# Halved doubled loads, a second late row buffer and re-measured planner figures in a spectral-mix and expert-retrieval kernel

## The chip, the cores and the metric

The kernel runs on one core of a Trainium2 chip. The core has a matrix engine (PE, with its weight loads shown apart as PEld), a vector engine (DVE), a scalar engine (ACT), a general engine (POOL, which here issues the gathers) and a queue engine (SP, which issues the plain loads and stores); all transfers run on 16 DMA engines. The metric is device time in microseconds, the median of several runs of the whole program.

## The reference

x has 2048 rows of 576 numbers. The result is a gated sum of two branches of the same x:

```
g   = sigmoid((x * gate_w).sum(-1))
a   = irfft2(rfft2(x) * (w_r + 1j * w_i))
q   = x @ w_q                          # 32 heads, two halves of 128 each
i1  = argmax over 64 of q1 . k1,  i2 = argmax over 64 of q2 . k2
e   = 64 * i1 + i2                     # one of 4096 rows per head
b   = sum over heads of gelu(x . u[e]) * v[e]
out = g * a + (1 - g) * b
```

With one candidate for each head the softmax is one. Branch a is a two-dimensional Fourier filter, written as products with cosine and sine tables. Branch b needs, for each of 2048 rows and 32 heads, one row of u and one row of v.

## The kernel before

**Tiles.** x is cut into 16 tiles of 128 rows. For branch b the 32 heads are cut into 8 chunks of 4. A *group* is one tile and one chunk: 4 gathers (one for each head; a gather fetches 128 rows of 4608 bytes, u and v side by side), 4 dot products with x on DVE (line 496, `group`), a gelu on ACT (line 500), and then the sum of the 4 v rows. That sum is done on DVE (line 514, four multiply-adds) or, where `is_d` says so, on PE by four diagonal matrices (`dg`, line 524) and eight products of 288 columns. There are 128 groups. Tiles 0 to 9 (`E_T`) are early: their 80 groups run beside the scores. Tiles 10 to 15 (`L_SEQ`) are late: their 48 groups, in which PE groups and DVE groups alternate, run beside the Fourier branch.

**Scores.** For each chunk `build_m` multiplies w_q by the keys; `scores` multiplies x by that, and DVE and ACT find the index of the largest score. The products are done on numbers cut in two parts (`load_x` makes a high part on ACT, line 361, and a low part on DVE, line 362). The last 64 columns of x are loaded twice, onto partitions 0 to 63 and 64 to 127, in blocks of 512 rows: 20 loads.

**Fourier branch.** When all score work is over, its memory is given to the second half (`switch`). `fold` (16 tiles) brings x into the buffer BT. Ten `unit` calls then do the Fourier transform over rows, the filter (`f4`, `f5`) and the way back (`f6`, `unit_back`) for two of 16 residues at a time. When all units are through, `invert` (16 tiles) does the last transform with a second table (`fi[1]`, line 640) and `mix` (line 835) adds both branches and stores.

**Row buffers.** Gathers land in a ring of 12 buffers (`uv`, NG), which also serves the loads of x and w_q in the scoring part. After `switch` one more buffer (`uv2`, NG2) serves gathers alone. A buffer is taken when the gather is issued, and is free again when the last reader of its v row (DVE or PE) is through.

**The order.** Every instruction stands in a list of jobs with a due time (`at`) and an assumed duration. `Plan.order` goes through time: whenever an engine is free it takes, among the jobs whose inputs are there and for which a buffer is free, the one that is due first. The order that comes out of it is fixed in the program; on the chip each engine then works in that order and waits where an input is late. So the assumed durations move no instruction of themselves, they change the order. They come from `dve`, `act`, `pe` (a product of n columns) and `load`; a gather is assumed to hold the DMA engines for `move` = 1.65 us, one after another. The due times of the late half: T0 is 636.8 in the list's own time; the late groups are due at T0 + 10 + 6.6 n (TLAG, TGS); fold n at T0 - 15 + 1.3 FPACE n; unit k at T0 + 20.8 FPACE + 14 FPACE k; inverse n 4.2 FPACE apart behind the units.

Of the kernel before, what the change touches and what calls it, by code (L numbers as in the profile page):

```python
# [32 lines left out]
def _tables():  # L33
# [10 lines left out]
    def rows(fn, ds):  # L44
        return fn(2 * np.pi * np.outer(ds, k) / D)

    z = np.zeros((P, DF))
    ct = z.copy()
# [4 lines left out]
    fwd = np.stack([  # L53
        rows(np.cos, np.arange(0, 128)), rows(np.cos, np.arange(128, 256)), ct,
        -rows(np.sin, np.arange(0, 128)), -rows(np.sin, np.arange(128, 256)), -st,
    ])
    ck = np.full(DF, 2.0)
    ck[0] = ck[-1] = 1.0
    ck /= S * D

    def irows(fn, ks):
        return fn(2 * np.pi * np.outer(ks, k) / D) * ck[ks][:, None]

    ct = z.copy()
    ct[:33] = irows(np.cos, np.arange(256, 289))
    st = z.copy()
    st[64:96] = irows(np.sin, np.arange(256, 288))
    inv = np.stack([
        irows(np.cos, np.arange(0, 128)), irows(np.cos, np.arange(128, 256)), ct,
        irows(np.sin, np.arange(0, 128)), irows(np.sin, np.arange(128, 256)), st,  # L70
# [12 lines left out]
        "t_fi": c(np.concatenate([fwd, inv]).transpose(1, 0, 2)),  # L83
        "t_f4": c(f4),
        "t_f6": c(f6),
# [158 lines left out]
def pe(n):  # L244
    return max(0.25, n * 0.0018)
# [7 lines left out]
def tile_kernel(ctx, tc, xn, xT, wqT, kT, wri, uv, gw, t_kr, t_fi, t_f4, t_f6, t_io, out):  # L253
# [84 lines left out]
    gate = pp.tile([P, NT], F32, tag="gate", name="gate")  # L338
    gone = pp.tile([P, NT], F32, tag="gone", name="gone")
# [16 lines left out]
    def load_x(b, i, at, at2):  # L356
        st = buf("uv", ROW, view=lambda x: x[:, 0, :512])
        ld(load(P * 2048, 2048), at, lambda: nc.sync.dma_start(st.ap, xT[:, i, b * 512 : b * 512 + 512]), [st])
        hi = xts[i if i < 4 else 8][b]
        lo, r = (xts[4 + i][b], 0) if i < 4 else (hi, 64)  # L360
        ac(act(512), at2, lambda: actv(hi.ap, st.ap, AF.Copy), [hi], [st])
        dv(dve(512), at2, lambda: vt(lo.ap[r:], st.ap[r:], hi.ap[r:].bitcast(F32), ALU.subtract), [lo], [st, hi])
# [117 lines left out]
    def group(t, c, at, ahead, gate_by=()):  # L480
        rows = []
        for k in range(HPC):
            g = buf(("uv", "uv2"), ROW)
            h = c * HPC + k

            def go(g=g, h=h):
                on("POOL", nc.gpsimd.indirect_dma_start(  # L487
                    out=g.ap.rearrange("p a d -> p (a d)"), out_offset=None, in_=uv,
                    in_offset=bass.IndirectOffsetOnAxis(ap=ei[t // 2][:, t % 2, h : h + 1], axis=0)))
# [124 lines left out]
    for tag, pool, n in (  # L614
            ("t2", "ip", NT2), ("bt", "ip", 1), ("fi1", "ip", 1), ("krb", "ip", 1),
            ("uv2", "x2", NG2), ("xl", "x2", NT - NE), ("gr", "x2", 1),
            ("f5", "fp", 2), ("kr", "fp", 1), ("fi0", "fp", 1), ("t4", "fp", 2), ("t6", "fp", 2), ("w", "fp", 2)):
# [14 lines left out]
    fi = [buf("fi0", [P, 6, DF]), buf("fi1", [P, 6, DF])]  # L632
# [5 lines left out]
    ld(load(P * 6936, 4096), T0 + 8, lambda: nc.sync.dma_start(fi[0].ap, t_fi[:, 0:6, :]), [fi[0]])  # L638
    ld(0.5, T0 + 15, lambda: nc.sync.dma_start(gw2.ap, gw.partition_broadcast(P)), [gw2])
    ld(load(P * 6936, 4096), T0 + 90, lambda: nc.sync.dma_start(fi[1].ap, t_fi[:, 6:12, :]), [fi[1]])  # L640
# [23 lines left out]
    def f2(q, at):  # L664
        p = psum()

        def go():
            for r in range(2):
                for n, i in enumerate(((0, 1, 2), (3, 4, 2))[r]):
                    mm(p.ap[:, r, :DF], BT.ap[:, i, :, q], fi[0].ap[:, 3 * r + n, :], start=n == 0, stop=n == 2)  # L670

        plan("PE", 6 * pe(DF), at, go, [p], [fi[0], (BT, "q", q)] + [(BT, "in", t, i) for t in range(NT) for i in range(2)])
# [4 lines left out]
    def turns(k, at):  # L677
        t4 = buf("t4", [P, 3, P])
        t6 = buf("t6", [P, 5, P])
        ld(load(P * 1024, 1024), at - 8, lambda: nc.sync.dma_start(t4.ap[:, 0:2, :], t_f4[k]), [(t4, 0)])  # L680
        ld(load(P * 1024, 1024), at - 8, lambda: nc.sync.dma_start(t6.ap[:, 0:2, :], t_f6[k]), [(t6, 0)])
        ac(act(128), at - 2, lambda: actv(t4.ap[:, 2, :], t4.ap[:, 1, :], AF.Copy, scale=-1.0), [(t4, 1)], [(t4, 0)])
        ac(act(256), at - 2, lambda: actv(t6.ap[:, 2:5:2, :], t6.ap[:, 0:1, :].to_broadcast([P, 2, P]), AF.Copy), [(t6, 1)], [(t6, 0)])
        ac(act(128), at - 2, lambda: actv(t6.ap[:, 3, :], t6.ap[:, 1, :], AF.Copy, scale=-1.0), [(t6, 2)], [(t6, 0)])
        tabs[k] = t4, t6

    def f4(k2, X, at):
# [4 lines left out]
        t4, t6 = tabs[min(k2, 16 - k2)]  # L692
        a, b = (1, 2) if k2 <= 8 else (2, 1)
        p = psum()

        def go():
            T, x, o = t4.ap, X.ap, p.ap
            mm(o[:, 0, :DF], T[:, 0, :], x[:, 0, :], start=True, stop=False)
            mm(o[:, 0, :DF], T[:, a, :], x[:, 1, :], start=False, stop=True)
            mm(o[:, 1, :DF], T[:, 0, :], x[:, 1, :], start=True, stop=False)  # L700
            mm(o[:, 1, :DF], T[:, b, :], x[:, 0, :], start=False, stop=True)

        plan("PE", 4 * pe(DF), at, go, [p], [X, (t4, 0), (t4, 1)])
# [226 lines left out]
```

## Time and profile before

| | us |
|---|---|
| median of 3 runs (lowest, highest) | 991.58 (990.01, 991.66) |
| the profiled execution, its own time | 1001.24 |
| span of its trace, first to last instruction | 999.5 |
| DVE busy in the span | 916.7 |
| PE busy in the span | 904.4 |
| last score product on PE starts | 601.4 |
| first product of the folds | 628.6 |
| first inverse | 862.7 |
| last product of an inverse | about 973 |

The profiled execution is 9.7 us (1.0%) longer than the median of the runs. A page of the profile gives for each engine its busy time; matmuls are shown with a modelled end that overlaps the next one, so their mean duration is longer than their pace. A window view gives the busy time of each engine in a stretch, with the number of instructions in brackets. A view of waits says which engine sat idle until which other instruction was done. Times in the trace count from the first instruction.

### The profile page before, as it was taken

How to read it: one execution, taken by the hardware profiler on the slowest of the kernel's cores; microseconds unless marked ns; L12 is line 12 of the kernel's file. 1: busy time of each engine (PE TensorE's matmuls, PEld its weight loads, DVE VectorE, ACT ScalarE, POOL GpSimd, SP SyncE). 2: the span in 40 equal slices, each digit the busy share in tenths (PEclk: the TensorE clock that was granted, in tenths of full speed). 3: DMA queues.
4: the chain of work that ended last, by engine and by line, in shares of the span. 5: the costliest groups of instructions: out<-in, count | busy, mean ns of one | idle time of the engine just before them, and what ended most of it. 6: DMA issues, size and time to landing. Idle time of an engine off the chain costs nothing. (4 is left out here: it accounts for less than half of the span.)

```text
span 999.5 us, 14406 instructions
## 1 busy us (share of the span) xinstructions
PE 904.4 (90%) x4208; PEld 735.8 (74%) x4208; DVE 916.7 (92%) x2255; ACT 514.6 (51%) x1877; POOL 574.4 (57%) x516
## 2 busy tenths in 40 slices
PE   8997999999999999999998990777999998899993
PEld 7885888878877888887877880665777776677762
DVE  3996999999999999999999999999999999977776
ACT  3874676676666576676666664522212222233331
POOL 0354656565656565755657566476655565676662
PEclk9997999999999999999999996889999999899998
DMA  9987999998989999998999799889999999999994
GB/s 336 336 286 301 349 361 367 358 352 305 392 309 361 371 344 332 395 345 328 386 360 330 291 394 378 340 312 389 394 357 351 357 353 321 349 390 414 398 359 192
DMA packets 93246, 348.39 MB, mean 349 GB/s; under 512 B 10480, under 2 KB 13296, under 8 KB 93168
## 3 DMA queue, kind: packets, MB, share of 16 engines
q0 software_dynamic: 73728, 302.02, 80.9%
q1 hardware_dynamic: 19440, 45.45, 12.3%
q8 instruction: 34, 0.56, 0.2%
q14 instruction: 44, 0.36, 0.1%
HBM read 342.71 MB, written 4.72 MB: 348 GB/s over the span
## 5 line engine op out<-in xcount | busy, mean ns | idle before, releaser
L487 POOL DMA_INDIRECT uv<-uv,ei x512 | 574.2, 1121 | 406.2 <-PE p L313 133.3
L313 PE MATMUL p<-mh,xt 128*128 128x512 f32 x1152 | 383.3, 402 | 9.1 <-ACT sg L435 7.3
L435 ACT ACTIVATE sg<-p,mx 128x64 bf16<-128x64 f32 x1024 | 225.8, 352 | 78.1 <-DVE mx L427 55.7
L514 DVE SCALAR_TENSOR_TENSOR xn<-uv,a,xn 128x576 f32<-128x576 f32 x322 | 262.0, 814 | 1.5
L313 PEld LDWEIGHTS p<-mh,xt 128*128 128x128 f32 x1152 | 218.4, 190 | 59.5 <-ACT sg L435 7.7
L313 PE MATMUL p<-ml,xt 128*128 128x512 f32 x640 | 253.2, 396 | 0.0
L496 DVE SCALAR_TENSOR_TENSOR uv<-uv,xn 128x576 f32<-128x576 f32 x320 | 236.3, 749 | 8.7 <-DMA uv<-uv,ei 6.8
L313 PE MATMUL p<-uv,dg 128*128 128x288 f32 x720 | 194.0, 425 | 29.3 <-ACT dg L524 22.5
L313 PEld LDWEIGHTS p<-uv,dg 128*128 128x128 f32 x720 | 140.8, 199 | 77.9 <-ACT dg L524 29.3
L496 DVE SCALAR_TENSOR_TENSOR uv<-uv,xl 128x576 f32<-128x576 f32 x192 | 141.5, 751 | 0.2
L313 PEld LDWEIGHTS p<-ml,xt 128*128 128x128 f32 x640 | 121.6, 190 | 26.6
L500 ACT ACTIVATE b<-z 128x4 f32<-128x4 f32 x128 | 26.4, 206 | 204.9 <-DVE uv L496 171.4
L313 PE MATMUL p<-fi,bt 128*128 128x289 f32 x384 | 97.7, 408 | 4.4 <-DVE t L710 3.0
L313 PEld LDWEIGHTS p<-fi,bt 128*128 128x128 f32 x384 | 83.5, 242 | 16.5 <-issue 3.7
L313 PEld LDWEIGHTS p<-kT,uv 128*128 128x128 f32 x640 | 77.8, 195 | 7.9 <-issue 4.8
L313 PE MATMUL p<-kT,uv 128*128 128x128 f32 x640 | 78.5, 279 | 5.0 <-DMA uv<-wqT 5.0
L427 DVE TENSOR_REDUCE mx<-p 128x16 f32<-128x1024 f32 x64 | 77.5, 1211 | 3.2 <-PE p L313 3.0
L313 PE MATMUL p<-t,t 128*128 128x289 f32 (+2 forms) x384 | 73.8, 362 | 5.9 <-issue 3.4
L446 ACT ACTIVATE sg<-sg 128x256 bf16<-128x256 bf16 x192 | 72.3, 427 | 1.2
L313 PEld LDWEIGHTS p<-t,t 128*128 128x128 f32 (+1 forms) x384 | 54.1, 165 | 23.9 <-issue 10.7
L524 ACT ACTIVATE dg<-ident,a 128x128 f32<-128x128 f32 x180 | 57.6, 393 | 17.7 <-DVE a L501 14.8
L313 PE MATMUL p<-kr,f 128*128 128x128 f32 x160 | 23.0, 301 | 31.5 <-ACT f L648 26.8
(86 smaller groups left out, 612.1 us busy)
## 6 DMA issues: line engine op xcount, KB each, us to landing
uv<-wqT SPq DMA_DIRECT2D x40, 512.0 KB
uv<-uv,ei POOLq DMA_INDIRECT x512
uv<-xT SPq DMA_DIRECT2D x20, 256.0 KB
w<-wri SPq DMA_DIRECT2D x16, 289.0 KB
out<-xn SPq DMA_DIRECT2D x16, 288.0 KB
xn<-xn SPq DMA_DIRECT2D x10, 288.0 KB
t<-t_f SPq DMA_DIRECT2D x18, 128.0 KB
fi<-t_fi SPq DMA_DIRECT2D x2, 867.0 KB
```

Source lines behind the costliest of these rows:

```text
L313: after("PE", nc.tensor.matmul(*args, **kw))
L427: dv(dve(1024, True), at, lambda: nc.vector.tensor_reduce(mv.ap[:, 2 * tp : 2 * tp + 2, :], ps.ap.rearrange("p a (g e) -> p a g e", e=E), ...
L435: on("ACT", actv(sg.ap[:, j, g, :], ps.ap[:, j, g * E : g * E + E], AF.Sign, bias=mv.ap[:, 2 * tp + j, g : g + 1], scale=-1.0))
L446: ac(act(256), at, lambda b=b: actv(s2()[:, :, b * Q : b * Q + Q], s2()[:, :, b * Q : b * Q + Q], AF.Copy, bias=b / 4), [sg], [])
L487: on("POOL", nc.gpsimd.indirect_dma_start(out=g.ap.rearrange("p a d -> p (a d)"), out_offset=None, in_=uv, in_offset=bass.IndirectOffsetOn ...
L496: dv(0.68, at, lambda k=k, g=rows[k]: stt(g.ap[:, 0, :], g.ap[:, 0, :], 1.0, x.ap, op0=ALU.mult, op1=ALU.mult, accum_out=z.ap[:, k : k + 1 ...
L500: ac(0.18, at - 9, lambda: actv(b.ap, z.ap, AF.Gelu_apprx_tanh), [b], zk, table="gelu")
L514: dv(0.73, at, lambda v=v, s=s: stt(y.ap, v(), s(), y.ap, op0=ALU.mult, op1=ALU.add), [y], [(rows[k], 1), a])
L524: ac(0.3, at - 9, lambda k=k, dg=dg: actv(dg.ap, ident, AF.Copy, scale=a.ap[:, k : k + 1]), [dg], [a, "ident"])
```

## The change

- **x.** The last 64 columns are loaded once, as an array of 64 partitions (`x5`); the low part is written by DVE onto partitions 64 to 127. Row blocks 2 and 3 are loaded together, so 20 loads of 256 KB become 8 of 256 KB, 4 of 512 KB, 2 of 128 KB and 1 of 256 KB. Block 3's conversion was due at 45.1 in the list, and is now due at 24 with block 2's. w_q's last columns stay doubled.
- **Tables.** One table `fi` serves both ways of the transform along the columns. The scale moves into a factor of the fold (2.0) and into `gsc`, the gate times 2/(S D), one small DVE instruction more; signs change places in the subtractions. Two loads of 867 KB become one.
- **Turning tables.** `t4` and `t6` (two loads of 128 KB each step) become `tw` (one load of 256 KB): 18 loads become 9, the same bytes. The copies on ACT stay three a step.
- **Buffers.** NG2 goes from 1 to 2.
- **Planner.** `pe(n)` becomes 0.01 + 0.00168 n (0.225 us for 128 columns instead of 0.25, 0.496 for 289 instead of 0.520); a gather's `move` becomes 1.55; FPACE goes from 1.7 to 1.4.

```diff
 def pe(n):
-    return max(0.25, n * 0.0018)
+    return 0.01 + n * 0.00168
...
-    def load_x(b, i, at, at2):
-        st = buf("uv", ROW, view=lambda x: x[:, 0, :512])
-        ld(load(P * 2048, 2048), at, lambda: nc.sync.dma_start(st.ap, xT[:, i, b * 512 : b * 512 + 512]), [st])
-        hi = xts[i if i < 4 else 8][b]
-        lo, r = (xts[4 + i][b], 0) if i < 4 else (hi, 64)
-        ac(act(512), at2, lambda: actv(hi.ap, st.ap, AF.Copy), [hi], [st])
-        dv(dve(512), at2, lambda: vt(lo.ap[r:], st.ap[r:], hi.ap[r:].bitcast(F32), ALU.subtract), [lo], [st, hi])
+    def load_x(b, i, at, at2, n=1):
+        st = buf("uv", ROW, view=lambda x: x.rearrange("p a d -> p (a d)")[:, : n * 512])
+        h = P if i < 4 else E
+        src = lambda: xT[:, i, b * 512 : (b + n) * 512] if i < 4 else x5[:, b * 512 : (b + n) * 512]
+        ld(load(h * n * 2048, n * 2048), at, lambda: nc.sync.dma_start(st.ap[:h], src()), [st])
+        for m in range(n):
+            hi = xts[i if i < 4 else 8][b + m]
+            lo, r = (xts[4 + i][b + m], 0) if i < 4 else (hi, E)
+            cut = lambda m=m: st.ap[:h, m * 512 : m * 512 + 512]
+            ac(act(512), at2, lambda hi=hi, cut=cut: actv(hi.ap[:h], cut(), AF.Copy), [hi], [st])
+            dv(dve(512), at2, lambda hi=hi, lo=lo, cut=cut: vt(lo.ap[r : r + h], cut(), hi.ap[:h].bitcast(F32), ALU.subtract), [lo], [st, hi])
...
-            plan("POOL", 1.13, at - ahead, go, [(g, 0), (g, 1)], [("ei", t // 2, c)], move=1.65, after=gate_by)
+            plan("POOL", 1.13, at - ahead, go, [(g, 0), (g, 1)], [("ei", t // 2, c)], move=1.55, after=gate_by)
...
-        load_x(2, i, 15, 24)
+        load_x(2, i, 15, 24, 2)
...
-    for i in range(ND):
-        load_x(3, i, 34, when(3))
...
-    fi = [buf("fi0", [P, 6, DF]), buf("fi1", [P, 6, DF])]
+    fi = buf("fi", [P, 6, DF])
...
-    ld(load(P * 6936, 4096), T0 + 90, lambda: nc.sync.dma_start(fi[1].ap, t_fi[:, 6:12, :]), [fi[1]])
...
-        ac(0.17, at, lambda: actv(f.ap[:, 0:385:384], x.ap[:, 0:1].to_broadcast([P, 2]), AF.Copy), [(f, 0)], [x])
+        ac(0.17, at, lambda: actv(f.ap[:, 0:385:384], x.ap[:, 0:1].to_broadcast([P, 2]), AF.Copy, scale=2.0), [(f, 0)], [x])
...
-        t4 = buf("t4", [P, 3, P])
-        t6 = buf("t6", [P, 5, P])
-        ld(load(P * 1024, 1024), at - 8, lambda: nc.sync.dma_start(t4.ap[:, 0:2, :], t_f4[k]), [(t4, 0)])
-        ld(load(P * 1024, 1024), at - 8, lambda: nc.sync.dma_start(t6.ap[:, 0:2, :], t_f6[k]), [(t6, 0)])
+        tw = tabs[k] = buf("tw", [P, 8, P])
+        ld(load(P * 2048, 2048), at - 8, lambda: nc.sync.dma_start(tw.ap[:, 1:5, :], t_tw[k]), [(tw, 0)])
...
+        dv(0.1, at, lambda: nc.vector.tensor_scalar(gsc, gate, 2.0 / (S * D), None, op0=ALU.mult), ["gsc"], ["gate"])
...
-NG2 = 1
+NG2 = 2
...
-FPACE = 1.7
+FPACE = 1.4
```

More of the change, by code (lines that the diff above doesn't have):

```diff
@@ L47, in _tables @@
     z = np.zeros((P, DF))
+    c0 = rows(np.cos, np.arange(0, 128))
+    c0[0] *= 0.5
     ct = z.copy()
@@ L52, in _tables @@
     st[64:96] = rows(np.sin, np.arange(256, 288))
[L53 to L70, printed above, removed]
+    fi = np.stack([
+        c0, rows(np.cos, np.arange(128, 256)), ct,
+        rows(np.sin, np.arange(0, 128)), rows(np.sin, np.arange(128, 256)), st,
     ])
@@ L252, in tile_kernel @@
 @with_exitstack
-def tile_kernel(ctx, tc, xn, xT, wqT, kT, wri, uv, gw, t_kr, t_fi, t_f4, t_f6, t_io, out):
+def tile_kernel(ctx, tc, xn, xT, x5, wqT, kT, wri, uv, gw, t_kr, t_fi, t_tw, t_io, out):
     nc = tc.nc
@@ L338, in tile_kernel @@
     gate = pp.tile([P, NT], F32, tag="gate", name="gate")
+    gsc = pp.tile([P, NT], F32, tag="gsc", name="gsc")
     gone = pp.tile([P, NT], F32, tag="gone", name="gone")
```

82 lines of the change are left out of this document (40 added, 42 removed).

## The prediction

> **What bounds the kernel now.** I read the page's busy line first, then a view of windows cut where the kernel changes its work, then the waits of POOL and DVE, and last the chain of waits and the rows of PE in the stretch that sets the end.
>
> ```profile
> PE 904.4 (90%) x4208; PEld 735.8 (74%) x4208; DVE 916.7 (92%) x2255; ACT 514.6 (51%) x1877; POOL 574.4 (57%) x516
> q0 software_dynamic: 73728, 302.02, 80.9%
> ```
>
> No engine stands out: DVE and PE are both over 90%, and the gathers alone hold the DMA engines for 80.9% of 999.5 us, 808.6 us, or 1.58 us for each of 512 gathers. An average over the span hides which one ends last, so I cut it:
>
> ```profile
> core 0: us, PE busy (x) PEld busy (x) DVE busy (x) ACT busy (x) POOL busy (x), PEclk, DMA share, GB/s
> 0.00:36.00 36.00, 31.04 (x176) 27.42 (x177) 17.79 (x34) 19.14 (x49) 0.20 (x4) 1.00 0.95 344
> 36.00:100.00 64.00, 56.48 (x265) 46.15 (x263) 54.23 (x141) 41.53 (x159) 33.52 (x32) 0.92 0.83 298
> 100.00:600.00 500.00, 490.21 (x2324) 401.90 (x2323) 489.13 (x1229) 333.80 (x1295) 305.56 (x269) 0.99 0.94 351
> 600.00:628.00 28.00, 1.84 (x8) 1.14 (x7) 27.89 (x68) 13.09 (x54) 19.48 (x17) 0.60 1.01 382
> 628.00:700.00 72.00, 56.69 (x285) 47.95 (x286) 69.00 (x181) 26.77 (x89) 41.91 (x37) 0.89 0.92 345
> 700.00:862.00 162.00, 148.24 (x677) 119.61 (x675) 157.47 (x373) 37.79 (x123) 95.09 (x89) 0.98 0.97 357
> 862.00:974.00 112.00, 109.93 (x448) 84.58 (x448) 84.43 (x198) 38.35 (x101) 73.18 (x67) 1.00 1.00 383
> 974.00:999.50 25.50, 9.98 (x32) 7.00 (x32) 16.80 (x38) 4.14 (x14) 5.41 (x5) 0.84 0.50 196
> ```
>
> From 100 to 862 DVE sets the pace (489.13 of 500; 157.47 of 162 in the units). Behind the last unit, from 862, PE does (109.93 of 112) while DVE idles for 27.6 us, and behind the last inverse nothing is full. So the end hangs on how the 48 late groups are shared between the stage in which DVE is full and the one in which PE is. The groups are counted by the one small DVE instruction that each has (line 501), with its windows in the order 628 to 700, 700 to 862, 862 to 974, 974 to the end:
>
> ```profile
> 628.00:700.00 72.00, 1.56 (x10) 0.89 0.92 345
> 700.00:862.00 162.00, 3.40 (x22) 0.98 0.97 357
> 862.00:974.00 112.00, 2.64 (x16) 1.00 1.00 383
> 974.00:999.50 25.50, 0.65 (x4) 0.84 0.50 196
> ```
>
> Twenty groups are still to come when the units end. Why no more have come shows in POOL's waits, first from 628 to 862, then (last line) from 862 on:
>
> ```profile
> POOL uv L487 <- PE p L313: 42.0, 18, 5.2
> POOL uv L487 <- DVE xn L514: 23.7, 16, 4.9
> ...
> POOL uv L487 <- PE p L313: 20.1, 10, 3.4
> ```
>
> POOL stands 65.7 of 234 us waiting for PE or DVE to give a row buffer back. In the units it issues 89 gathers in 162 us, one in 1.82 us; with the inverses 67 in 112, one in 1.67.
>
> **What one group and one inverse cost.** From the chain, three dots in 2.04 us and one multiply-add; from PE's rows, a cycle of two inverses and one PE group:
>
> ```profile
> 649.42 2.04 DVE uv L496 x6
> 671.41 0.73 DVE xn L514
> ...
> 885.26 6.01 PE L313 MATMUL p<-fi,bt 128*128 128x289 f32 x24
> 891.23 2.22 PE L313 MATMUL p<-t,krb 128*128 128x289 f32 x8
> 893.29 4.04 PE L313 MATMUL p<-uv,dg 128*128 128x288 f32 x16
> 897.17 2.11 PE L313 MATMUL p<-t,krb 128*128 128x289 f32 x8
> 899.12 6.02 PE L313 MATMUL p<-fi,bt 128*128 128x289 f32 x24
> ...
> 862.68 107.72 PE p L313 x440
> 990.51 0.66 ACT xn L538
> 995.54 0.82 DVE xn L835
> ```
>
> A dot paces at 0.68 us. A group is 4 x 0.68 on DVE, plus 4 x 0.73 for every second group, plus about 0.08 for line 501: 4.26 us of DVE on the mean. On PE a group's products take 897.17 - 893.29 = 3.88 us, again for every second group: 1.94. Two inverses take 899.12 - 885.26 - 3.88 = 9.98, one 4.99, all 16 together 79.8.
>
> Behind 862 there are then 79.8 + 20 x 1.94 = 118.6 us of PE, and 72 gathers (67 + 5); measured are 990.5 - 862 = 128.5 us to the last product, and 9.0 of drain behind it (one gated sum, four multiply-adds, one more gated sum, the store). 128.5 over 20 groups is 6.4 us a group. So the stage is held by the flow of groups, with PE 10 us behind; they would be equal where 79.8 + 1.94 g = 6.4 g, at g = 17.9 groups.
>
> **The change part by part.**
>
> *Loads at the start.* The sizes and counts, the first gather, and DVE's longest kind of wait between 36 and 100:
>
> ```profile
> uv<-xT SPq DMA_DIRECT2D x20, 256.0 KB
> t<-t_f SPq DMA_DIRECT2D x18, 128.0 KB
> fi<-t_fi SPq DMA_DIRECT2D x2, 867.0 KB
> 36.67 1.07 POOL L487 DMA_INDIRECT uv<-uv,ei  x1 [36.22 <-ACT cand L472]
> DVE a L501 <- ACT b L500: 8.0, 2, 4.8
> ```
>
> The last columns' 128 KB are dropped once for each of four row blocks, 0.52 MB; at 344 GB/s that is 1.5 us of a stage whose DMA share is 0.95. Fifteen buffer turns of the shared ring replace twenty. Against it, five conversions (0.67 us on ACT, 0.69 on DVE by the rows below) move ahead of the index work that the first gather waits for at 36.67. If all of them came before it, that is 3.4 us on each engine; none need, since the index of the first tile is due at 16 and the conversions at 24. Between 36 and 100 DVE idles 9.8 us, 8.0 of it in two waits that this reordering may deepen or remove. Bounds: -8.0 (both waits go) to +11.4 (both double, and all conversions first); I take -1, the bytes with a third given back, as the list's own order by due time keeps the conversions behind.
>
> ```profile
> L361 ACT ACTIVATE xt<-uv 128x512 fp32r<-128x512 f32 x20 | 12.4, 668 | 7.9 <-DMA uv<-xT 7.9
> L362 DVE TENSOR_TENSOR xt<-uv,xt 128x512 fp32r<-128x512 f32 x16 | 10.8, 687 | 12.4 <-ACT xt L361 12.4
> L804 DVE TENSOR_SCALAR gone<-gate 128x16 f32<-128x16 f32 x1 | 0.4, 391 | 0.0
> DVE uv L496 <- DMA uv<-uv,ei: 6.8, 10, 1.2
> ```
>
> [...]
>
> *Tables.* 0.89 MB and ten issues on SP less, in a stage of 382 GB/s: 2.3 us of DMA. No engine waits for it: DVE waited for gathers 6.8 us in the whole span, and the second table was issued at 628, 235 us before its first use. Zero; if the DMA engines were the bound, -2.3. `gsc` is one instruction like L804's, 0.4 us at the most, at 710 in a full DVE: +0.2 to +0.4. The factors and exchanged subtractions cost nothing, they change no count and no shape.
>
> *Scoring, 100 to 600.* New order, same work. DVE has 10.9 us of idle to win there, and as much could be lost in new misfits; -5 to +5, I take 0, because nothing is added or removed and 97.8% is already full.
>
> *Row buffer, `move`, `pe`, FPACE.* These act together on g, the groups left at the end of the units. More flow: with 13 buffers and a gather each 1.82 us, a buffer is held 23.7 us; 14 held as long give one each 1.69 us, and with the inverses 1.67 x 13/14 = 1.55. In the units that is up to 162/1.69 = 96 gathers instead of 89, under two groups. The assumed gather time falls by 0.1, 0.4 a group, so the list sees less reason to hold groups back. Against it, FPACE brings the units forward: the first unit's due time falls by 6.2 us, each step from 23.8 to 19.6, so that the last unit is due at T0 + 205.5 instead of T0 + 249.6, and by due times 30 groups lie ahead of it instead of 36. In the trace only 28 did (48 - 20), so the due times were not what limited them; the flow was. Now both say about the same: 30 groups by due time, 28 + 7/4 by flow. I take g = 18.5, between 16 (1.55 us a gather in the units too, 104 gathers) and 26 (units first, below).
>
> The sum on the profile's own time: 1.5 groups more before 862 cost 1.5 x 4.26 = 6.4, DVE being full there; units end at 868.4. Behind it PE has 79.8 + 18.5 x 1.94 = 115.7, the gathers 74 x 1.55 = 114.7; PE decides. Of the 10 us in which PE waited I keep 1. End of products 985.1, drain 9.0: 994.1, against 999.5: -5.4. With -1 at the start, +0.3 for `gsc` and -1 for tables (between 0 and -2.3, as DMA share is 1.00 in 862 to 974): -7.1. The profiled execution took 1001.24 us; the median of the runs is 991.58, so I carry the difference over: **984.5 us**. Its own range is 979 to 989.
>
> **Rivals.**
>
> *Units first, a tail of groups (slower).* FPACE wins over the flow: unit jobs, now due 6 to 44 us earlier, take DVE from the groups. Place: line 514 and 496 between 700 and 862. Price: a group that is moved behind the units saves 4.26 and costs 6.4, 2.1 us each, from 20 left on; at g = 26 the units end at 836.4, the rest takes 166.4, the end is 1011.8, less 1.7 for loads and tables 1010.1: +10.6, **1002 us**; it decides from g over 20. For it: the groups' own due times are unchanged while everything they compete with moves ahead. Against: the groups already run late on their due times, and late jobs go first.
>
> *PE full, nothing won.* The groups flow as fast as the buffers let them, g falls to 15; units end at 883.3, PE then has 108.9, the drain 9.0: 1001.2, less 1.7 for the loads and tables: **991.5 us**. For it: DVE is full in the units, so each group costs its 4.26 there and spares PE only 1.94. Against: it needs five groups more, 20 gathers, and the buffer alone gives 7. It is also the case in which a part does not do what it says: an extra buffer only holds rows longer.
>
> *DVE full to the end (better).* The 101.2 us that DVE is busy behind 862 run at 97%, as in the units: 104 + 9, end 975, **967 us**. Against: PE has 118.6 there; 15 us would have to go into PE's idle time before 862 (15.3 and 13.8 us).
>
> *The start stalls (slower).* The conversions come ahead of the first indices and the two waits double: +11.4, with the 6.1 won behind +5.3, **997 us**. For it: the first gather came at 36.67, 7.5 us behind its due time in the list (16 + 2.8 x 9.7 - 14 = 29.2), so conversions due at 24 can be ready before the index chain is through. Against: fewer buffer turns in the ring.
>
> **How the numbers follow.** Forecast 0.42; units first 0.20; PE full 0.16; DVE full 0.14; start 0.08. Faster by over 0.2% (2 us; about what a measurement of this kernel tells from no change): 0.42 + 0.14 + 0.06 of PE full, 0.62. Within: 0.10 of PE full. Slower: 0.20 + 0.08, 0.28. The range 971 to 1001 leaves out the outer half of DVE full and of units first, and takes in the start's worst case and scoring's 5 us either way.
>
> **What would show it.** Right: POOL's waits for PE and DVE between 628 and the end of the units fall from 66 us by a quarter; 18 or 19 of line 501 behind the last unit; PE in one piece through the inverses with a PE clock of 1.00; the end within 10 us of the last product. Wrong: over 20 groups left, and DVE and POOL alone busy behind the last inverse (units first); units ending after 880 (PE full); the first gather after 40, or a wait over 5 us before 100 (start).

## The result and the profile after

The changed kernel took 994.79 us, the median of 6 runs (991.44 to 996.30); the kernel before, run beside it, 991.50 us (987.98 to 992.66). The ratio is 1.0038, with an interval from 1.0022 to 1.0055: a little slower. The forecast was 984.5 us, faster. The profiled execution after took 994.56 us with a span of 992.7 us, an ordinary one of its runs.

The first view is the busy line of the page after, then windows from 36 us to the end, cut in the late half where the first product of a fold starts (627.7), where the units end (867.5) and where the last inverse ends (978.5). The columns are those of the prediction's windows; line numbers differ from kernel to kernel, the names of the tiles don't.

```profile
PE 898.4 (91%) x4208; PEld 731.0 (74%) x4208; DVE 913.3 (92%) x2256; ACT 516.8 (52%) x1877; POOL 578.0 (58%) x516
```

```profile
36.00:100.00 64.00, 62.25 (x309) 51.42 (x308) 61.61 (x160) 45.73 (x171) 39.55 (x35) 1.00 0.87 333
100.00:600.00 500.00, 482.26 (x2292) 394.60 (x2290) 483.37 (x1216) 333.43 (x1287) 295.84 (x266) 1.00 0.93 347
600.00:627.70 27.70, 0.04 (x1) 0.04 (x1) 27.70 (x71) 13.18 (x53) 18.96 (x17) 0.52 0.98 373
627.70:700.00 72.30, 60.50 (x300) 52.07 (x301) 68.01 (x176) 25.81 (x90) 47.90 (x41) 0.90 0.93 350
700.00:867.50 167.50, 149.06 (x677) 118.01 (x676) 164.69 (x399) 39.23 (x127) 107.63 (x95) 0.97 0.99 374
867.50:978.50 111.00, 109.54 (x449) 84.61 (x448) 85.66 (x203) 39.32 (x104) 67.89 (x62) 1.00 0.96 375
978.50:992.70 14.20, 4.32 (x18) 3.03 (x16) 6.23 (x11) 1.75 (x4) 0.00 (x0) 0.79 0.11 42
```

The same windows with only the small DVE instruction that each group has (line 492 of this kernel), and POOL's waits between the folds and the end of the units:

```profile
627.70:700.00 72.30, 1.66 (x11) 0.90 0.93 350
700.00:867.50 167.50, 3.49 (x23) 0.97 0.99 374
867.50:978.50 111.00, 2.73 (x17) 1.00 0.96 375
978.50:992.70 14.20, 0.16 (x1) 0.79 0.11 42
```

```profile
POOL uv L478 <- PE p L299: 35.0, 24, 4.9
POOL uv L478 <- DVE xn L505: 13.3, 18, 4.9
```

The last steps of PE in the chain of waits, start and duration in us:

```profile
868.25 107.74 PE p L299 x440
976.72 6.11 PE p L299 x24
```

The late half came out as the sum had it: 18 groups left (17 + 1) when the units end at 867.5, where 18.5 and 868.4 were forecast; POOL's waits for PE and DVE fell from 65.7 to 48.3 us; PE runs in one piece behind the units, at a PE clock of 1.00; the last product ends at 976.72 + 6.11 = 982.8 (985.1 was forecast), 9.9 us ahead of the end; and the span is 992.7 where the sum gave 999.5 - 7.1 = 992.4. Judged by that trace alone the forecast holds. But the kernel is not faster, so the trace of before can't stand for the timed runs of before. The kernel before was therefore profiled again on the chip of another run of the changed kernel. Here are the windows of that trace of before, cut at its own landmarks (folds 620.0, units' end 849.8, last inverse 960.6), and DVE's longest wait up to the folds:

```profile
36.00:100.00 64.00, 61.94 (x306) 50.92 (x306) 61.68 (x158) 47.44 (x183) 38.51 (x35) 1.00 0.90 336
100.00:600.00 500.00, 483.05 (x2291) 395.50 (x2289) 489.83 (x1233) 331.27 (x1279) 308.44 (x270) 0.99 0.94 353
...
36.00:620.00 584.00, 545.00 (x2595) 446.42 (x2594) 571.51 (x1439) 390.21 (x1509) 361.42 (x317) 0.98 0.94 353
...
620.00:849.80 229.80, 201.96 (x960) 165.48 (x960) 224.37 (x547) 64.36 (x209) 136.91 (x126) 0.97 0.96 355
849.80:960.60 110.80, 109.34 (x449) 84.64 (x448) 85.54 (x201) 38.03 (x99) 72.64 (x66) 1.00 1.00 387
960.60:987.00 26.40, 10.28 (x34) 6.99 (x32) 16.80 (x38) 4.70 (x15) 6.13 (x6) 0.85 0.52 207
```

```profile
DVE uv L496 <- DMA uv<-uv,ei: 7.3, 12, 1.9
```

And the same two views of the changed kernel on that chip (folds 628.0, units' end 867.1, last inverse 978.1):

```profile
36.00:100.00 64.00, 61.65 (x305) 50.98 (x304) 60.98 (x157) 45.04 (x169) 39.14 (x35) 1.00 0.85 322
100.00:600.00 500.00, 482.32 (x2293) 394.76 (x2291) 483.00 (x1216) 333.38 (x1287) 293.85 (x266) 1.00 0.92 347
...
36.00:628.00 592.00, 544.01 (x2598) 445.79 (x2596) 571.98 (x1442) 391.89 (x1507) 352.83 (x317) 0.98 0.92 345
...
628.00:867.10 239.10, 209.44 (x976) 169.92 (x976) 232.52 (x574) 65.04 (x214) 154.74 (x135) 0.95 0.97 367
867.10:978.10 111.00, 109.54 (x449) 84.61 (x448) 85.71 (x203) 39.33 (x104) 67.90 (x62) 1.00 0.96 376
978.10:992.40 14.30, 4.32 (x18) 3.04 (x16) 6.24 (x11) 1.75 (x4) 0.00 (x0) 0.80 0.11 41
```

```profile
DVE uv L487 <- DMA uv<-uv,ei: 14.8, 18, 1.6
```

Between 36 and 100 the profile that the prediction was built on has DVE busy for 54.23 of 64 us at a PE clock of 0.92; this one has 61.68 at 1.00. That execution took longer than every timed run made beside it (987.98 to 992.66 us), and 7.5 of the 8.6 us by which its folds start later than here are in this one stage. Against the second trace the change reads differently. From the folds to the end it wins 367.0 - 364.4 = 2.6 us. Up to the folds it loses 8.0 (628.0 against 620.0), and there DVE does the same work, 571.98 against 571.51 us; what grows is its idle time, from 12.5 to 20.0 us, and the waits for gathers in it, from 7.3 to 14.8. Of the 7.5 us more, 6.8 come between 100 and 600 (17.0 idle against 10.2) and 0.7 ahead of it. The spans differ by 5.4 us, the medians of the two pairs by 3.3 and 3.8.

### The profile page after: what moved, and what is told of

Its sections match the earlier page's. It is cut to its first block, busy times and chain, and to the rows that moved or that the text cites. A ratio compares the mean times of both kernels' runs of the same rounds, so it can differ in the third digit from the quotient of the medians.

```text
span 992.7 us, 14381 instructions
## 1 busy us (share of the span) xinstructions
PE 898.4 (91%) x4208; PEld 731.0 (74%) x4208; DVE 913.3 (92%) x2256; ACT 516.8 (52%) x1877; POOL 578.0 (58%) x516
## 4 chain that ended last, share of the span: by engine, by line
DVE 48%; PE 36%; DMA 9%; issue 4%; POOL 1%; ACT 1%; SPq 0%; POOLq 0%; ACTq 0%; DVEq 0%
PE p L299 36%; DVE uv L487 17%; DVE xn L505 12%; DMA uv<-uv,ei 8%; DVE mx L418 4%; DVE sg L439 2%; POOL uv L478 1%; DVE im L442 1%; DVE ml L388 1%; DVE t L695 1%; DVE t L696 1%; DVE sg L440 1%; DVE xn L531 1%; DMA uv<-wqT 1%; DVE a L492 1%
## 5 line engine op out<-in xcount | busy, mean ns | idle before, releaser
L299 PE MATMUL p<-uv,dg 128*128 128x288 f32 x720 | 190.3, 419 | 27.3 <-ACT dg L515 20.6
L487 DVE SCALAR_TENSOR_TENSOR uv<-uv,xl 128x576 f32<-128x576 f32 x192 | 139.1, 750 | 2.0 <-DMA uv<-uv,ei 1.7
L299 PE MATMUL p<-kr,f 128*128 128x128 f32 x160 | 22.2, 298 | 31.5 <-ACT f L636 30.2
L299 PEld LDWEIGHTS p<-kr,f 128*128 128x128 f32 x160 | 20.8, 208 | 33.2 <-ACT f L636 30.8
L439 DVE TENSOR_TENSOR sg<-sg 128x512 bf16<-128x512 bf16 (+1 forms) x128 | 43.7, 348 | 0.0
## 6 DMA issues: line engine op xcount, KB each, us to landing
uv<-xT SPq DMA_DIRECT2D x4, 512.0 KB, 10.9
```

Source lines behind the costliest of these rows:

```text
L299: after("PE", nc.tensor.matmul(*args, **kw))
L439: dv(0.07 + wd * 16 / 1920, at, lambda wd=wd: vt(s2()[:, :, :wd], s2()[:, :, :wd], s2()[:, :, wd : 2 * wd], ALU.min), [sg], [])
L487: dv(0.68, at, lambda k=k, g=rows[k]: stt(g.ap[:, 0, :], g.ap[:, 0, :], 1.0, x.ap, op0=ALU.mult, op1=ALU.mult, accum_out=z.ap[:, k : k + 1 ...
```

## The experiments

Ratios are to the kernel before, run in turn with the kernel on the same chip; intervals are 95%. There are five groups of runs on four chips: e1 to e4 on A, e5 to e8 on B, e9 to e12 on C, e13 to e16 on A again, e17 and e18 on D. On chips B and C the kernel before took 991.25 and 990.49 us, on D 999.09, on A 1007.11 in the first group and 999.45 in the second, so times of different chips aren't compared. The table gives for each profile the start of the first fold product; DVE's busy and idle time from 36 us to there; the two stretches behind (folds to units' end, and on to the end); and the groups left at the units' end. "Before" and "after" are unchanged kernels.

| run, chip | ratio (interval) | first fold | DVE busy, idle | units | behind | left |
|---|---|---|---|---|---|---|
| e1 before, A | 1.0016 (0.9990 to 1.0043) | 630.9 | 571.7, 23.2 | 233.5 | 143.4 | 20 |
| e6 before, B | 0.9979 (0.9951 to 1.0006) | 620.0 | 571.5, 12.5 | 229.8 | 137.2 | 20 |
| e5 after, B | 1.0034 (1.0010 to 1.0058) | 628.0 | 572.0, 20.0 | 239.1 | 125.3 | 18 |
| e8 old loads of x, B | 1.0012 (0.9990 to 1.0034) | 629.8 | 572.0, 21.8 | 238.5 | 125.4 | 18 |
| e7 old `move`, B | 1.0095 (1.0058 to 1.0132) | 626.2 | 572.5, 17.7 | 239.7 | 131.3 | 18 |
| e3 old `pe` and `move`, A | 1.0043 (1.0015 to 1.0071) | 631.8 | 570.5, 25.3 | 242.0 | 131.1 | 19 |
| e2 FPACE 1.7, A | 1.0196 (1.0161 to 1.0231) | 650.5 | 572.7, 41.9 | 265.0 | 116.4 | 14 |
| e4 one late buffer, A | 1.0166 (1.0113 to 1.0218) | 650.1 | 573.6, 40.6 | 246.9 | 126.7 | 18 |
| e9 after, scores ordered as before, C | 0.9993 (0.9978 to 1.0008) | 619.0 | 570.7, 12.3 | 243.5 | 125.9 | 18 |
| e10 after, old figures in scores, C | 1.0027 (1.0008 to 1.0046) | 622.2 | 570.0, 16.2 | 240.3 | 125.8 | 18 |
| e11 after, old `pe` in scores, C | 1.0348 (1.0326 to 1.0370) | 657.9 | 574.5, 47.4 | 240.9 | 125.2 | 18 |
| e12 before, new figures in scores, C | 1.0139 (1.0116 to 1.0161) | 629.6 | 571.9, 21.7 | 232.2 | 139.3 | 20 |
| e13 before, `move` 1.75 in scores, A | 1.0127 (1.0081 to 1.0174) | 636.4 | 571.8, 28.6 | 223.9 | 149.6 | 22 |
| e14 before, ACT + 2 ns in scores, A | 1.0166 (1.0124 to 1.0208) | 638.5 | 571.0, 31.5 | 232.4 | 140.4 | 20 |
| e15 before, NG2 2 and FPACE 1.4, A | 1.0082 (1.0053 to 1.0111) | 625.6 | 571.5, 18.1 | 236.6 | 138.7 | 20 |
| e16 as e9, FPACE 1.55, A | 1.0064 (1.0031 to 1.0097) | 621.0 | 570.5, 14.5 | 271.0 | 112.3 | 14 |
| e17 after, ACT + 2 ns in scores, D | 1.0096 (1.0056 to 1.0137) | 641.7 | 572.6, 33.1 | 248.6 | 125.2 | 18 |
| e18 before, ACT - 2 ns in scores, D | 0.9954 (0.9925 to 0.9983) | 622.6 | 573.0, 13.6 | 233.6 | 139.1 | 20 |

The column to read first is DVE's: its work up to the folds lies between 570.0 and 574.5 us whatever was done, and its idle time between 12 and 47. That idle time decides when the folds begin.

A profile is one execution. Those of B and C lie at most 2.9 us off the median of their kernel's runs, those of A up to some 5 us, and that of e17 lies 10.2 us above it. The traces from A and D, and the first profile of before, also lack part of the record: the landing times of the transfers, and about a fifth of the semaphore updates that tell who ended a wait (of DVE's, e1 has 1264 and e6, of the same kernel, 1644). Idle time can be trusted there; the name of what was waited for less so.

### Parts of the change taken back

Two unchanged kernels give the scatter of a profile. e1 is the kernel before on chip A, e6 on chip B, e5 the changed kernel on chip B. No diff.

> The kernel before, once more, with a second profile. Theory A: the first profiled execution of before (1001.24 us against a median of 991.5) had lost some 9 us between 36 and 100, where PE idled 7.5 us with a clock of 0.92; then the new span is 988 to 992, DVE is busy 61 to 62 of 64 us in 36 to 100 instead of 54.2, and the late half (from 628 on, 371.5 us there) has about the same length. Theory B: the first profile was typical and only longer as a whole; then 36 to 100 shows the same idle time. Ratio to before 1.000 within 0.002 in both.

> The kernel before, for a profile on the chip of the run above. Ratio 1.000. Its folds start at 628 to 632, and from there to the end it takes 370 to 377 us; the changed kernel should take 4 to 10 us less for that part in both theories, and more for the part ahead of it in theory A.

> The changed kernel as it is, with a profile beside one of the kernel before (next run) on one chip. The two runs with FPACE and the buffer undone have the same order of instructions as the changed kernel until the folds, yet their score part ended at 640 instead of 617 us, while the kernel before lost only 2 us on that chip against its first profile. Theory A: the changed order of the score part is the fragile one; on such a chip it loses some 20 us there itself, the late half wins about 6, and the ratio is 1.012 to 1.02; on a chip like the first it is 1.003 to 1.005. Theory B: those losses belonged to the undone parts; then the last score product comes at 598 to 602 and the ratio is 1.002 to 1.006 on any chip.

The ratio of the change repeated (1.0034 beside 1.0038). e6 came out below what was expected, with folds at 620.0 and not at 628 to 632. e1 did as its theory B says: its DVE idles 11.0 us between 36 and 100, like the first profile of before.

```profile
36.00:100.00 64.00, 55.07 (x259) 45.01 (x258) 53.04 (x138) 40.41 (x152) 32.37 (x30) 0.92 0.79 288
```

So the first profile was no single accident: it has the loss of e1, and the gaps in the record of all traces from A and D. In both, ACT stands between 36 and 100 before its copies of the score matrices (`mh`, line 396), 5.6 us in the first profile and 7.1 in e1, until something that the trace doesn't name. In e6, with the same order on PE, DVE and ACT, it doesn't stand there at all. On which chip the first profile was taken is not on record.

Late half: e2 and e4 each take one setting back.

```diff
-FPACE = 1.4
+FPACE = 1.7
```

> The changed kernel with FPACE back at 1.7. If FPACE put the units ahead and left groups for the end, undoing it gives the loss back: 0.995 to 1.000 of before, 17 or fewer groups left behind the last unit. If FPACE only made up for the larger flow of groups, undoing it leaves units later (after 870) and more PE work at the end: 1.005 to 1.010. If the start carries the loss, nothing changes: 1.003 to 1.005.

```diff
-NG2 = 2
+NG2 = 1
```

> The changed kernel with one late row buffer instead of two. If the buffer is worth what the prediction gave it (about two groups more by the end of the units, some 4 us), the ratio is 1.006 to 1.009 and POOL's waits for PE and DVE between 628 and 862 rise from 50 us towards 66. If it is worth nothing, the ratio stays 1.003 to 1.005.

Both ratios lie outside everything that was expected. Neither setting changes the order up to the folds, so 650.5 and 650.1 are the changed kernel's score order on chip A: 22 us later than on B, where before's order moved by 11. The ratios of both therefore say little of the late half; its stretches do. One buffer instead of two leaves 18 groups as well, with POOL's waits for PE and DVE at 60.0 us, as expected for it, so it wasn't the buffer that brought them forward. FPACE 1.7 with the new figures brings far too many forward: 14 left, 265.0 + 116.4 = 381.4 us against 373.6 in e4.

Planner and loads: e3 sets both figures back in the changed kernel, e7 only `move`, e8 only the loads of x.

```diff
-    return 0.01 + n * 0.00168
+    return max(0.25, n * 0.0018)
...
-move=1.55
+move=1.65
```

> The changed kernel with the old assumed durations (pe and a gather's move) and FPACE 1.4. If the new figures cost the time, since gathers assumed at 1.55 us are placed earlier than they land (DVE's waits for gathers rose from 6.8 to 15.1 us in the two traces), those waits fall to about 7 us and the ratio is 0.995 to 1.000. If the figures help, 1.005 to 1.010. If the start carries the loss, 1.003 to 1.005.

> The changed kernel with a gather's assumed time back at 1.65 us and nothing else undone. Theory A with the figure as its cause: builds of the score matrices no longer come ahead of late w_q loads, DVE's waits for gathers fall from 15 to about 6 us, the last score product comes at 600 to 605 on any chip, the late half keeps most of its gain, ratio 0.990 to 0.998. If the figure is not the cause, the ratio is that of the changed kernel within 0.003.

```diff
-        load_x(2, i, 15, 24, 2)
+        load_x(2, i, 15, 24)
...
+    for i in range(ND):
+        load_x(3, i, 34, when(3))
```

> The changed kernel with the loads of x as before (20 of 256 KB, block 3 converted late). If the larger and earlier loads cost the time at the start (the first gather came at 39.4 instead of 36.7 us), 0.003 to 0.006 below the changed kernel, with the first gather at 36 to 37. If they only save their bytes, 0.000 to 0.002 above it.

e3 and e4, on one chip, differ by 18 us at the folds: there the figures cost, not the rest. e3's waits for gathers did fall, to 5.9 us, but its ratio stayed at 1.0043. e7's ratio, 1.0095, lies outside both expectations, and its waits for gathers fell only to 11.8. Its folds are still 6.2 us late on B, and behind them it loses another 4 us against before (371.0 to 367.0). e8 brings the first gather back to 36.8 us, from 38.8, but not the folds (629.8); its profiled execution is the longest of its runs, 2.7 us above their median. Its interval overlaps that of e5, so whether the loads cost 2 us or none stays open.

### The score part by itself

A flag, set back where the late half begins to be planned, gives the score part other figures than the rest. e9 has the old loads too; its PE, DVE and ACT work in exactly the order of before up to the folds. e10 keeps the new loads, e11 the new `move` as well; e12 is the mirror image, the kernel before with the new figures in the scores alone.

```diff
 def pe(n):
-    return 0.01 + n * 0.00168
+    return max(0.25, n * 0.0018) if SCORES[0] else 0.01 + n * 0.00168
...
-move=1.55
+move=1.65 if SCORES[0] else 1.55
...
     T0 = when(NCH * 8)
+    SCORES[0] = False
```

> The changed kernel, but x is loaded as before and the order of the score part is made with the figures of before (fp32 products 0.25 and 0.52 us, a gather 1.65); the late half keeps the new figures, FPACE 1.4 and two late buffers. The score part then has exactly the order of before. Theory A (the change loses about 8 us in the score part through its new order, and wins about 2.6 us from the folds on): folds begin where those of the kernel before do on this chip, within 2 us, and the stretch from the first fold to the end is 2 to 4 us shorter than the kernel before's; ratio 0.997, between 0.995 and 0.999. Rival B (a score part that ends earlier only meets the same DMA and DVE limits later, so that the late half gives nothing by itself): ratio 0.999 to 1.002, the late half as long as before's. Rival C (the loss comes from the start or from something else that the change adds, not from the order): ratio 1.003, folds 6 to 8 us late.

> The changed kernel with its new loads of x, but the order of the score part is made with the figures of before; the late half keeps the new figures. Theory A (the planner's figures make the loss, the loads of x do not): DVE's waits for gathers in the score part about half of the changed kernel's 16 us, folds within 2 us of the kernel before's, ratio 0.996 to 0.999, like the run with the old loads. Rival C (the loads of x and the conversions moved ahead make the loss): ratio 1.002 to 1.005 and folds 6 to 8 us late, first gather about 2 us late.

> The changed kernel, but in the score part the products are planned with the figure of before (0.25 us for 128 columns, 0.92 for 512) while a gather is planned with the new 1.55. Theory A1 (the products' figure makes the loss): folds within 2 us of the kernel before's, ratio 0.996 to 0.999. Theory A2 (the gather's figure makes the loss): folds 6 to 8 us late, ratio 1.002 to 1.005. If every order but that of before loses the same (A3, an order made by hand for one set of figures), this run too loses 5 us or more.

> The kernel before, with the new figures of products and gathers in the score part alone; loads, late buffer, FPACE and the late half as before. Theory A (the figures make the loss in the score part): folds 6 to 9 us later than the kernel before's on this chip, DVE's waits for gathers 14 to 16 us instead of 7, ratio 1.006 to 1.009. Rival C (the loads of x make it): ratio 0.999 to 1.002.

For e9, e12 and e11, in this order, the window up to the folds and DVE's first wait in it:

```profile
36.00:619.00 583.00, 545.88 (x2595) 447.84 (x2593) 570.73 (x1439) 390.40 (x1508) 359.96 (x317) 0.97 0.94 352
```

```profile
DVE uv L487 <- DMA uv<-uv,ei: 6.7, 10, 1.7
```

```profile
36.00:629.60 593.60, 545.37 (x2597) 446.99 (x2595) 571.90 (x1443) 392.71 (x1509) 353.65 (x317) 0.98 0.93 348
```

```profile
DVE uv L500 <- DMA uv<-uv,ei: 13.5, 19, 1.7
```

```profile
36.00:657.90 621.90, 558.13 (x2598) 455.69 (x2596) 574.51 (x1441) 390.59 (x1511) 360.75 (x317) 0.95 0.89 329
```

```profile
DVE uv L491 <- DMA uv<-uv,ei: 34.4, 37, 2.8
DVE xn L535 <- PE p L303: 9.1, 6, 2.4
```

With before's order the loss is gone (e9; the changed kernel itself wasn't run on C), and the two figures alone, with nothing else of the change, make it (e12: 10.6 us more up to the folds than e9 on the same chip, 9.4 of it DVE idle). The traces have one more test of it: up to the folds e8 and e12 turn out to have one order on PE, DVE and ACT. They start the folds at 629.8 on B and 629.6 on C, where the order of before has 620.0 (e6) and 619.0 (e9), although e8 has the late half of the change and e12 that of before. So the start of the folds goes with the order. This settles where the loss is. But e11 spoils the simple reading: the new `move` without the new `pe` costs far more than both, 36 us against e10, while the new `pe` alone (e7) costs no more than both up to the folds (626.2 against 628.0). A figure's size doesn't say what it costs. e9, e10, e11 and e12 also came out above what was expected. e10's folds start at 622.2, but its profiled execution lies 2.9 us below the median of its runs, and its ratio is 1.0027: that the loads of x cost nothing isn't shown. e9's ratio is 0.9993 and not 0.997: the late half wins less there, with DVE waiting longer for the gelus between 619.0 and 862.5 than the changed kernel did in its units on chip B (1.9 us):

```profile
DVE a L492 <- ACT b L491: 5.7, 6, 2.3
```

### Is it the figures, or any other order?

e13 gives a gather more slack than before; e14, e17 and e18 move the planned duration of every ACT instruction in the scores by 2 ns, which changes the order on DVE, ACT and PE in many places and takes no slack from gathers or products. e14 (0.167) and e18 (0.163) start from the kernel before, e17 (0.167) from the changed one.

```diff
-move=1.65
+move=1.75 if SCORES[0] else 1.65
```

> The kernel before, with a gather assumed to hold the DMA engines for 1.75 us instead of 1.65 in the score part; nothing else. Theory S (the new figures lose because they take the slack out of the order; the measured share of the queue is 1.58 us a gather, 1.65 left 0.07 and 1.55 leaves less than nothing): more slack does no harm, folds within 2 us of the kernel before's, DVE's waits for gathers 7 us or less, ratio 0.997 to 1.002. Theory T (the order of before is one good draw among many, and nearly every other order is worse): folds 4 to 15 us later, ratio 1.004 to 1.015.

```diff
 def act(n):
-    return 0.165 + n / 1200
+    return (0.167 if SCORES[0] else 0.165) + n / 1200
```

> The kernel before, with every instruction of ACT in the score part planned 2 ns longer (0.167 instead of 0.165 us plus its length); nothing else. The order of DVE, ACT and PE changes in many places, the slack for gathers and products does not. Theory S: folds within 2 us of the kernel before's, ratio 0.998 to 1.002. Theory T: folds 4 to 15 us later, ratio 1.004 to 1.015, DVE's waits for gathers over 10 us.

> The changed kernel, with every instruction of ACT in the score part planned 2 ns longer (0.167 us plus its length); nothing else. Theory T (each order is a draw, and the one of the changed kernel is a middling one): ratio to the kernel before anywhere from 0.998 to 1.025, more than 0.003 away from the changed kernel's 1.0036 on either side. Theory U (the new figures themselves are what is wrong, whatever the order): ratio 1.001 to 1.006, folds within 2 us of the changed kernel's 628.

> The kernel before, with every instruction of ACT in the score part planned 2 ns shorter (0.163 us plus its length); nothing else. Theory T: slower, ratio 1.003 to 1.025, folds 3 to 20 us later than the kernel before's. If only a longer figure for ACT harms (it is what puts the gelus and signs late in the list): ratio 0.997 to 1.002.

DVE's waits up to the folds in e15 (described below; it has before's order of the scores, and ran in the same group on the same chip), then in e13 and in e14:

```profile
DVE uv L496 <- DMA uv<-uv,ei: 6.7, 11, 1.4
DVE a L501 <- ACT b L500: 5.3, 5, 2.3
DVE xn L540 <- PE p L313: 1.3, 2, 0.9
```

```profile
DVE a L505 <- ACT b L504: 11.4, 7, 3.1
DVE xn L544 <- PE p L317: 9.2, 5, 2.5
DVE uv L500 <- DMA uv<-uv,ei: 1.9, 2, 1.3
```

```profile
DVE a L505 <- ACT b L504: 10.1, 5, 3.8
DVE uv L500 <- PE p L317: 7.2, 4, 2.5
DVE xn L544 <- PE p L317: 6.3, 4, 2.5
DVE uv L500 <- DMA uv<-uv,ei: 5.0, 9, 1.0
```

More slack did to the gathers what it should, 1.9 us of waits instead of 6.7, and the kernel became 1.3% slower, because the wait moved: DVE waits 11.4 us for ACT's gelus instead of 5.3, and 9.2 for PE instead of 1.3. So it isn't slack for gathers that makes the order of before fast. In e14, with no figure of a gather or a product touched, the same two waits grow to 10.1 and 7.2 + 6.3. Two ns on ACT cost the kernel before 1.7% one way (e14, on A) and won it 0.5% the other (e18, on D): e18 is faster than the kernel before, where neither expectation had it. With the same 2 ns the changed kernel has 1.0096 on D (e17) beside 1.0034 without them on B. The changed kernel itself was not run on D, and its order lost 22 us more on A than on B, so this difference may be the chip's.

The order of the scores is a draw. Nine orders other than before's were run: the changed kernel's own, that of e3 and e10, that of e8 and e12, and those of e7, e11, e13, e14, e17 and e18. The kernels with the first eight have ratios between 1.0012 and 1.0348, and e18 has 0.9954. e18 is the only version that beat the kernel before, and on chip D alone; beside the changed kernel it was not run.

### The late half by itself

e15 gives the kernel before two late buffers and FPACE 1.4 and nothing else; e16 is e9 with another pace.

```diff
-NG2 = 1
+NG2 = 2
...
-FPACE = 1.7
+FPACE = 1.4
```

> The kernel before with two late row buffers and FPACE 1.4; its loads, tables and the planner's figures as they were, so the score part has the order of before. If the late half of the change wins by itself: 18 or 19 groups left at the end of the units, first fold to end 2 to 4 us shorter than the kernel before's, ratio 0.995 to 0.999. If it does not, as the earlier run with the old order of the scores suggests: first fold to end within 3 us, ratio 0.999 to 1.003.

```diff
-FPACE = 1.4
+FPACE = 1.55
```

> The changed kernel with the old loads of x and the order of the score part made with the old figures (ratio 0.9993 before), and FPACE 1.55 instead of 1.4. Between 1.4 (18 groups left) and 1.7 (14 left, and slower): 16 or 17 groups left. If 1.4 is the better side of an optimum near 18 groups: the stretch from first fold to end 3 to 8 us longer, ratio 1.002 to 1.008. If the waits of DVE for ACT's gelus in the units are only a misfit of one order: ratio 0.996 to 0.999.

The late half of e16 in two windows, up to the units' end and behind it:

```profile
621.00:892.00 271.00, 225.06 (x1008) 179.63 (x1008) 252.95 (x623) 69.81 (x228) 166.64 (x150) 0.92 0.95 358
892.00:1004.30 112.30, 105.79 (x432) 81.56 (x432) 71.13 (x164) 37.60 (x95) 50.77 (x46) 1.00 0.76 295
```

With the old figures the second buffer and the pace leave 20 groups, as before, and the kernel is slower (e15; its profiled execution, with a span of 1000.9 us, is among the fastest of its runs, 1001.0 to 1012.6, so the profile doesn't show where its median of 1006.9 loses; its ratio lies outside both expectations). With both figures old 19 or 20 groups are left (e3, e15), with the new `pe` 18, also with one buffer (e4) and with the old `move` (e7). So one group goes with the product figure (e3 to e7), and one with the rest of the change (e15 to e3). At 14 groups (e16, where 16 or 17 were expected) DVE idles 18.1 us in the units, and the late half takes 383.3 us against 375.3 in e15 on the same chip.

What the late half of the change is worth, first fold to end, chip by chip: on B 364.4 and 363.9 against 367.0; on C 369.4, 366.1 and 366.1 against 371.5 with before's late half; on D 373.8 (e17) against 372.7 (e18), where e17's profiled execution is too far above its median to tell. A gain of 2 to 5 us on two chips, from single executions that lie up to 2.9 us off their medians. In e9's median no gain is left that could be told from none.

## Why the prediction was wrong

**The bound: right.** DVE up to the units' end (164.69 of the last 167.5 us), then PE (109.54 of 111.0). It holds more strictly than stated: DVE's work up to the folds is nearly a constant (570.0 to 574.5 us), and the idle time between (12 to 47 us) makes the difference.

**Groups left and units' end: right in number, wrong in cause.** 18 for 18.5, 867.5 for 868.4. The prediction let the second buffer's flow carry them; e4 has the same 18 without it. POOL's waits fell by 26%, as said, and that was beside the point.

**The prices: right.** Ahead of the units' end two groups and `gsc` cost DVE 232.52 - 224.37 = 8.2 us of work, where 2 x 4.26 + 0.3 = 8.8 was priced; the stretch grew by 9.3, with 1.2 more of idle time. Behind it the stretch shrank by 137.2 - 125.3 = 11.9, so 5.9 a group against 6.4. PE's 79.8 + 18 x 1.94 = 114.7 stands against 982.8 - 867.5 = 115.3 in the trace. The break-even near 18 groups isn't contradicted: at 14 the late half loses, at 20 a little.

**Start: wrong, and small.** "None need" come ahead of the first gather, I wrote of the conversions. Three did. The low parts of x on DVE up to 41 us, in the profile of before and in that of after:

```profile
L362 DVE TENSOR_TENSOR xt<-uv,xt x15: 678/690/693, 6.2 to 36.8; 128x512 fp32r<-128x512 f32 x12, 64x512 fp32r<-64x512 f32 x3
```

```profile
L353 DVE TENSOR_TENSOR xt<-uv,xt x18: 678/683/694, 6.6 to 40.3; 128x512 fp32r<-128x512 f32 x16, 64x512 fp32r<-64x512 f32 x2
```

```profile
L478 POOL DMA_INDIRECT uv<-uv,ei x1 | 2.5, 2542 | 39.0 <-DVE xt L353 39.0
```

18 instead of 15, three at 0.683 us, 2.0 us of the 11.4 that the worst case had; the first gather came at 39.4 instead of 36.7, and the last thing POOL waited for was such a conversion. e8, without this delay, has late folds too.

**Loads of 64 columns.** The trace now shows loads to 64 partitions beside those to 128, with KB and median us from issue to landing:

```profile
uv<-xT SPq DMA_DIRECT2D x8, 256.0 KB, 6.3
uv<-xT SPq DMA_DIRECT2D x4, 512.0 KB, 10.9
uv<-x SPq DMA_DIRECT2D x2, 128.0 KB, 7.3
uv<-x SPq DMA_DIRECT2D x1, 256.0 KB, 12.2
```

Half the bytes show 7.3 us instead of 6.3, and 12.2 instead of 10.9, but each load to 64 partitions is the last of its row block, behind the others in the queue, and the landing grows along the first block: its four loads of 256 KB land after 4.2, 5.8, 6.8 and 7.2 us, and the one to 64 partitions behind them after 8.8. At the same place the landing is the same: the fifth and the tenth load of x land after 7.6 and 6.5 us in e5, with 128 KB to 64 partitions, and after 7.6 and 6.5 in e6, with 256 KB to 128. In the first pair of profiles ACT, waiting for the fifth load, starts its conversion at 13.37 us after the change and at 12.54 before it, the load being issued at 4.6 in both. So the dropped bytes made these loads no faster. Whether they saved the loads behind them the estimated 1.5 us isn't shown by these landings.

**Scoring, 100 to 600: the step that failed.** "I take 0, because nothing is added or removed and 97.8% is already full." The bounds were -5 to +5; on B the stretch up to the folds lost 8.0 us, 6.8 of it as idle time of DVE between 100 and 600, and e12 lost 10.6 against e9. That DVE is full bounds only a gain: 10.9 us of idle time were left to win, but nothing bounds what a new order can lose. The step also put a change of figures in the class of things that move no work, when its whole effect is to draw a new order for 500 us.

**Carrying a difference from one execution to the median: the second fault.** The sum's 992.4 us met the span after, 992.7, because two errors of like size cancelled: the trace of before had its folds at 628.6, where traces of the same order on B and C have 620.0 and 619.0, and the change lost 8.0 there. The prediction noted that this execution lay 9.7 us above the median, and then took off 7.1 us from the median as if the surplus were spread over the whole span. On like traces the account is: forecast -7.1, measured +5.4; of the difference of 12.5, 9.0 is the scores and the start (+8.0 for -1), 3.5 the late half (-2.6 for -6.1).

**Rivals.** None was the case. "The start stalls" named something that did happen, at a sixth of its price; the loss lay in the place that none covered.

What stays open: why one order waits more than another. The waits move between gathers (34.4 us in e11), gelus (11.4 in e13) and PE (7.2 + 6.3 in e14) from draw to draw, and no single one was taken out alone.

## What to carry to other kernels

Where a planner writes a fixed order, a truer figure is not a better order: any edit to a duration redraws the order of a full stage, and the redraw is worth more, here -0.5 to +3.5%, than the edit. Price such an edit with the spread of a few meaningless ones, 2 ns here or there, and pick among the draws on more than one chip. And before a sum is made on one profile, see that its execution lies among the timed runs; if it doesn't, find the stage that holds the surplus, because a change can't win back there what an ordinary run doesn't lose.

## What the runs showed of the hardware

The same order took longer on one chip than on another. Up to the folds the changed order takes 628.0 us on chip B and 650.5 on A, and before's 620.0 on B and between 621.0 (e16) and 630.9 (e1) on A, with DVE's work the same to 2 us. The kernel before had medians from 990.49 to 1007.11 us on four chips, and 1007.11 and 999.45 in two groups on one. Where the chips differ can be seen in part: over the whole trace ACT stands before its copies of the score matrices (`mh`) for 17.7 us with the changed order on B (e5), but for 59.5 and 61.0 us with the same order on A (e2, e4), of which 16.2 and 33.5 are put down to nothing that the trace holds. With before's order it is 9.8 us on B (e6) and 23.9 on A (e1). What makes ACT wait there, and why the same traces lack part of their record, stays open.
